# Block-sparse attention and eight experts: expert tiles of 128 instead of 256 slots, the last seven under nested conditions

## The chip, the cores and the metric

One program on one core of a Trainium2 chip. The metric is the device time of the program in microseconds (us). The engines are TensorE (PE; its weight loads are a row of their own, PEld), VectorE (DVE), ScalarE (ACT), GpSimd (POOL) and SyncE (SP, which issues the transfers of weights). Matrix products read SBUF and write PSUM; VectorE and ScalarE carry results from PSUM back to SBUF.

## The reference

Two stages, all in f32. The first is masked attention (4 batches, 8 heads, 768 positions, heads of 64); the second sends each of the 3072 tokens, of width 512, to one of 8 experts:

```
xn = x / (norm(x) + 1e-6);  en = expert_emb / (norm(expert_emb) + 1e-6)
logits = xn @ en.T / tau
expert_idx = argmax(logits, axis=1)
gate_w = softmax(logits)[expert_idx]
for e in range(8):
    mask = expert_idx == e
    h = maximum(x[mask] @ w1[e], 0.0)          # w1[e]: 512 x 1024
    out[mask] = gate_w[mask] * (h @ w2[e])     # w2[e]: 1024 x 512
```

The inputs come from a fixed seed. With them the eight experts get 813, 192, 322, 753, 256, 320, 192 and 224 tokens.

## The kernel before

The program runs in four stretches: attention (`attention_fast`) with the router of each batch behind it (`route`), which writes the tokens and their gate weight as rows of 513 numbers to `x_dram`; then `dispatch`, which sorts the tokens into slots; then `experts`; last a condition on `good` (L635), whose body repeats everything in a safer form and is skipped with these inputs.

`dispatch` gives each expert whole tiles of `G` = 256 slots. Which expert a tile belongs to stands in `k.expert`, which token a slot holds in `k.slot` (an empty slot points at a row of zeros). Since the number of tiles that the experts fill is known only on the chip, the kernel always runs the most there can be, `NG` = (3072 + 8·255) // 256 = 19. With the counts above the experts fill 4 + 1 + 2 + 3 + 1 + 2 + 1 + 1 = 15 of them; the other 4 work on rows of zeros.

`experts` (L585) calls `fetch(i + 1)` and `expert_tile(i)` in turn. `fetch` (L465) loads the expert's number into a register of SP, and SP issues one transfer for `w1` (L469) and one for `w2` (L471), 2 MB each, into pools of two buffers; GpSimd gathers two times 128 rows of `x_dram` (L476). `expert_tile` (L485) makes on TensorE, one after the other: 8 transposes of 128x128 into PSUM (`xg_ps`, L491), 32 products `hp` with 256 columns (L502: 8 blocks of the hidden width times 4 of the depth), and two times 8 products `yp` with 512 columns (L510). The trace counts each f32 product as two instructions (a weight load and a matmul each), so a tile has 8 pairs of transposes, 64 pairs of `hp` and 32 of `yp`. Half of the transposed tokens is copied by DVE (L494), half by ACT (L495). `hp` uses a new PSUM buffer for each four blocks; ACT takes the relu of the first two blocks (L504) and DVE that of the other two (L505). DVE scales `yp` by the gate (L513), and GpSimd scatters the rows to the output (L515).

The Tile framework sets the order on each engine by a schedule, and adds a wait wherever two engines touch the same tile; the order below is what it made.

Of the kernel before, what the change touches and what calls it, by code (L numbers as in the profile page):

```python
# [406 lines left out]
def dispatch(k):  # L407

    nc, p = k.nc, k.dp
    cp = k.small.tile([P, 512], F32, name="cp", tag="small")  # L410
    nc.tensor.matmul(cp[:, 0:E], lhsT=k.ones, rhs=k.seen[:, NT, :], start=True, stop=True)
    cnt = p.tile([P, E], F32, name="cnt")
    nc.vector.tensor_copy(out=cnt, in_=cp[:, 0:E])

    more = p.tile([P, E, N // G], F32, name="more")
    nc.vector.tensor_tensor(out=more, in0=cnt.unsqueeze(2).broadcast_to([P, E, N // G]),
                            in1=k.by_g.unsqueeze(1).broadcast_to([P, E, N // G]), op=ALU.is_gt)
    need = p.tile([P, E], F32, name="need")
# [36 lines left out]

    ps = k.small.tile([P, 512], F32, name="slot_ps", tag="small")
    for t in range(NT):
        lane = p.tile([P, P], F32, name="lane_oh", bufs=4)
        nc.vector.tensor_scalar(out=lane, in0=k.lane, scalar1=low[:, t:t + 1], scalar2=None, op0=ALU.is_equal)
        nc.tensor.matmul(ps[:, 0:NS], lhsT=lane, rhs=val[:, t, :], start=(t == 0), stop=(t == NT - 1))  # L460
    k.slot = k.const.tile([P, NS], I32, name="slot")
    nc.vector.tensor_scalar(out=k.slot, in0=ps[:, 0:NS], scalar1=float(N), scalar2=None, op0=ALU.add)  # L462


def fetch(k, i):  # L465
    nc = k.nc
    e = nc.values_load(k.expert[0:1, i:i + 1], engines=(mybir.EngineType.SP,), min_val=0, max_val=E - 1)
    w1 = k.wp.tile([P, ND, F], F32, name="w1", tag="w1")
    nc.sync.dma_start(out=w1, in_=k.w1[bass.ds(e, 1), :, :].rearrange("o (c p) f -> p (o c) f", p=P))  # L469
    w2 = k.wp.tile([P, NF, DM], F32, name="w2", tag="w2")  # L470
    nc.sync.dma_start(out=w2, in_=k.w2[bass.ds(e, 1), :, :].rearrange("o (c p) m -> p (o c) m", p=P))  # L471
    xs = []
    for s in range(GS):
        x = k.gp.tile([P, XW], F32, name="xg", tag="xg")
        t = i * GS + s
        nc.gpsimd.indirect_dma_start(  # L476
            out=x[:, :], out_offset=None, in_=k.x_dram[:, :],
            in_offset=bass.IndirectOffsetOnAxis(ap=k.slot[:, t:t + 1], axis=0),
            bounds_check=N, oob_is_err=False,
        )  # L480
        xs.append(x)
    k.fetched[i] = (w1, w2, xs)


def expert_tile(k, i):  # L485
    nc = k.nc
    w1, w2, xs = k.fetched.pop(i)
    ps = k.big.tile([P, ND, GS, P], F32, name="xg_ps", tag="big")
    for d in range(ND):
        for s in range(GS):  # L490
            nc.tensor.transpose(ps[:, d, s, :], xs[s][:, d * P:(d + 1) * P], k.ident)  # L491
    xt = k.mp.tile([P, ND, G], F32, name="xgt", tag="xgt")
    half = ND // 2
    nc.vector.tensor_copy(out=xt[:, 0:half], in_=ps[:, 0:half].rearrange("p d s t -> p d (s t)"))  # L494
    nc.scalar.copy(out=xt[:, half:ND], in_=ps[:, half:ND].rearrange("p d s t -> p d (s t)"))  # L495

    h = k.mp.tile([P, NF, G], F32, name="h", tag="h")
    for f0 in range(0, NF, 4):
        hp = k.big.tile([P, 4, G], F32, name="hp", tag="big")
        for f in range(4):  # L500
            for d in range(ND):
                nc.tensor.matmul(hp[:, f, :], lhsT=w1[:, d, (f0 + f) * P:(f0 + f + 1) * P], rhs=xt[:, d, :],  # L502
                                 start=(d == 0), stop=(d == ND - 1))
        nc.scalar.activation(h[:, f0:f0 + 2], hp[:, 0:2], ACT.Relu)  # L504
        nc.vector.tensor_scalar(out=h[:, f0 + 2:f0 + 4], in0=hp[:, 2:4], scalar1=0.0, scalar2=None, op0=ALU.max)  # L505

    for s in range(GS):
        yp = k.small.tile([P, DM], F32, name="yp", tag="small")
        for f in range(NF):
            nc.tensor.matmul(yp, lhsT=h[:, f, s * P:(s + 1) * P], rhs=w2[:, f, :],  # L510
                             start=(f == 0), stop=(f == NF - 1))
        y = k.gp.tile([P, DM], F32, name="y", tag="y")
        nc.vector.tensor_scalar(out=y, in0=yp, scalar1=xs[s][:, DM:XW], scalar2=None, op0=ALU.mult)  # L513
        t = i * GS + s
        nc.gpsimd.indirect_dma_start(  # L515
            out=k.out[:, :], out_offset=bass.IndirectOffsetOnAxis(ap=k.slot[:, t:t + 1], axis=0),
            in_=y[:, :], in_offset=None, bounds_check=N - 1, oob_is_err=False,
        )
# [66 lines left out]
def experts(n):  # L585
    with ExitStack() as ctx:
        n.wp = ctx.enter_context(n.tc.tile_pool(name="wp", bufs=2))
        n.gp = ctx.enter_context(n.tc.tile_pool(name="gp", bufs=4))
        n.mp = ctx.enter_context(n.tc.tile_pool(name="mp", bufs=2))
        fetch(n, 0)  # L590
        for i in range(NG):
            if i + 1 < NG:
                fetch(n, i + 1)
            expert_tile(n, i)


@with_exitstack
def kernel(
# [23 lines left out]
    n.small = ctx.enter_context(tc.tile_pool(name="small", bufs=2, space=PSUM))  # L622
# [3 lines left out]
    with ExitStack() as attn:  # L626
        attention_fast(n, attn)
    n.big = ctx.enter_context(tc.tile_pool(name="big", bufs=3, space=PSUM))
    with tc.tile_pool(name="dp", bufs=1) as n.dp:
        dispatch(n)  # L630
        count_good(n)
    experts(n)

    good = n.nc.values_load(n.good[0:1, 0:1], min_val=0, max_val=N * H)
    with tc.If(good < N * H):  # L635
        n.exact = True
        with tc.tile_pool(name="const_x", bufs=1) as n.const_x, ExitStack() as attn:
            attention_exact(n, attn)
        with tc.tile_pool(name="dp_x", bufs=1) as n.dp:
            dispatch(n)  # L640
        experts(n)


# [30 lines left out]
```

## Time and profile before

| what | value |
|---|---|
| median of three runs | 1157.51 us (1157.3 to 1158.6) |
| the profiled execution | 1155.99 us, its span 1154.3 us |
| mean granted TensorE clock | 0.953 |
| PE busy | 1091.7 us (95%) |
| stretch of the experts | from 568 us to the end |

The page gives, for one execution, the busy time of each engine, the span in 40 slices, the chain of work that ended last and the costliest groups of instructions. A granted clock of 1.00 is 2.4 GHz, 0.50 is 1.2 GHz. A DMA share of 1.0 means that all 16 DMA engines were moving packets.

### The profile page before, as it was taken

The numbers are of one execution on the slowest core, as the hardware profiler recorded it, in microseconds if no ns is written. First come the engines' busy times: TensorE is split into PE (matmuls) and PEld (weight loads), VectorE is DVE, ScalarE is ACT, GpSimd is POOL, SyncE is SP. The second block draws the span as 40 slices with busy tenths as digits, with TensorE's granted clock in tenths as the row PEclk, the third lists the DMA queues.
The fourth block names the chain that finished last, engine by engine and source line by source line (L and its number), as shares of the span: only waits on it lengthen the run. The fifth ranks groups of instructions, "written<-read, shape, count | busy, mean of one in ns | idle before, by whom it ended". The sixth has DMA issues, their size and how long they took to land.

```text
span 1154.3 us, 12005 instructions
## 1 busy us (share of the span) xinstructions
PE 1091.7 (95%) x4938; PEld 617.5 (53%) x4938; DVE 309.8 (27%) x526; ACT 235.6 (20%) x370; POOL 93.3 (8%) x125
## 2 busy tenths in 40 slices
PE   5999999999999999998499999999999999999995
PEld 2444454445344454436466666666666666666662
DVE  3444434443344434434501111111111111111110
ACT  2443423343344413342000000000000000000000
POOL 1000010000000010000101111111111111111100
PEclk9999979998899969998589999999999999999998
DMA  6111111111211110000385554454444444454400
GB/s 151 42 42 41 42 69 41 42 42 28 96 41 42 42 55 14 1 2 7 144 305 182 182 182 165 170 174 159 173 171 173 175 177 166 175 181 164 165 1 3
DMA packets 91159, 122.05 MB, mean 106 GB/s; under 512 B 53324, under 2 KB 57420, under 8 KB 90582
## 3 DMA queue, kind: packets, MB, share of 16 engines
q1 hardware_dynamic: 85014, 104.90, 27.4%
q0 software_dynamic: 6080, 16.28, 4.0%
q8 instruction: 41, 0.67, 0.2%
q14 instruction: 24, 0.20, 0.0%
HBM read 108.56 MB, written 16.27 MB: 108 GB/s over the span
## 4 chain that ended last, share of the span: by engine, by line
PE 93%; DVE 2%; issue 2%; DMA 1%; SPq 1%; POOL 0%; POOLq 0%
PE hp L502 23%; PE yp L510 23%; PE sc L275 15%; PE av L295 14%; PE sc L272 5%; PE back L317 3%; PE turn L257 3%; PE lg L368 3%; PE xg_ps L491 2%; PE back L313 1%; DVE xgt L494 1%; PE xt_ps L363 1%; DMA xg<-x_dram,slot 1%; DVE xt L365 1%; SPq L173 1%
## 5 line engine op out<-in xcount | busy, mean ns | idle before, releaser
L502 PE MATMUL hp<-xgt,w 128*128 128x256 f32 x1216 | 270.1, 383 | 14.9 <-DVE xgt L494 14.1
L510 PE MATMUL yp<-w,h 128*128 128x512 f32 x608 | 264.0, 592 | 0.0
L502 PEld LDWEIGHTS hp<-xgt,w 128*128 128x128 f32 x1216 | 231.3, 191 | 50.7 <-DVE xgt L494 18.4
L278 ACT ACTIVATE e<-sc 128x768 f32<-128x768 f32 x192 | 155.4, 809 | 288.7 <-PE sc L275 288.7
L275 PE MATMUL sc<-qt,kt 64*128 64x384 f32 x768 | 192.7, 557 | 0.0
L510 PEld LDWEIGHTS yp<-w,h 128*128 128x128 f32 x608 | 115.5, 190 | 137.3 <-issue 136.3
L295 PE MATMUL av<-e,vld 128*64 128x384 f32 x768 | 173.5, 525 | 0.0
L293 DVE TENSOR_TENSOR esum<-esum,e 128x768 f32<-128x768 f32 x128 | 122.4, 956 | 106.0 <-ACT e L278 106.0
L505 DVE TENSOR_SCALAR h<-hp 128x512 f32<-128x512 f32 x38 | 26.3, 691 | 270.7 <-ACT h L504 270.7
L513 DVE TENSOR_SCALAR y<-yp,xg 128x512 f32<-128x512 f32 x38 | 28.5, 751 | 221.6 <-PE yp L510 221.6
L295 PEld LDWEIGHTS av<-e,vld 128*64 128x64 f32 x768 | 39.3, 137 | 81.9 <-issue 64.0
L275 PEld LDWEIGHTS sc<-qt,kt 64*128 64x128 f32 x768 | 62.7, 192 | 35.9 <-issue 35.8
L515 POOL DMA_INDIRECT out_dram<-y,slot x38 | 38.5, 1014 | 485.2 <-DVE y L513 485.2
L504 ACT ACTIVATE h<-hp 128x512 f32<-128x512 f32 x38 | 22.7, 597 | 247.7 <-PE hp L502 247.7
L272 PEld LDWEIGHTS <-kmask 24*128 24x128 bf16 x384 | 18.3, 91 | 102.7 <-issue 102.2
L495 ACT COPY xgt<-xg_ps 128x512 f32<-128x512 f32 x19 | 11.1, 585 | 299.9 <-DVE xgt L494 299.9
L272 PE MATMUL sc<-qmask,kmask 24*128 24x384 bf16 x384 | 66.5, 340 | 0.0
L291 DVE TENSOR_TENSOR esum<-e 128x768 f32<-128x768 f32 x32 | 30.7, 958 | 110.9 <-ACT e L278 110.9
L317 PEld LDWEIGHTS back<-ones,esum 128*128 128x128 f32 x384 | 45.4, 192 | 0.0
L317 PE MATMUL back<-ones,esum 128*128 128x1 f32 x384 | 44.7, 243 | 0.0
L354 POOL TENSOR_TENSOR nrm<-nrm,half 128x6 f32<-128x6 f32 x4 | 5.3, 1327 | 485.7 <-ACT sq L353 485.7
L476 POOL DMA_INDIRECT xg<-x_dram,slot x38 | 39.2, 1030 | 31.5 <-DVE slot L462 20.3
(124 smaller groups left out, 423.7 us busy)
## 6 DMA issues: line engine op xcount, KB each, us to landing
w<-in_moe_w_dram SPq DMA_DIRECT2D x38, 2048.0 KB, 9.3
x_dram<-x SPq DMA_DIRECT2D x4, 1539.0 KB, 5.8
kld<-in_k_dram SPq DMA_DIRECT2D x32, 192.0 KB, 3.1
qld<-in_q_dram SPq DMA_DIRECT2D x32, 192.0 KB, 3.2
vld<-in_v_dram SPq DMA_DIRECT2D x16, 384.0 KB, 3.1
xg<-x_dram,slot POOLq DMA_INDIRECT x38, 6.5
out_dram<-y,slot POOLq DMA_INDIRECT x38, 2.8
x_dram<-zero SPq DMA_DIRECT2D x1, 2.0 KB
```

Of the source, the lines that this page charges most:

```text
L257: nc.tensor.transpose(ps[:, c * P:(c + 1) * P], src[:, lo + c].rearrange("p h d -> p (h d)"), k.ident)
L272: nc.tensor.matmul(ps[:, h, 0:HALF], lhsT=k.kmask[32 * h:32 * h + NB, keys], rhs=k.qmask[32 * h:32 * h + NB, queries], start=True, stop=False)
L275: nc.tensor.matmul(ps[:, h, 0:HALF], lhsT=kt[D * h:D * (h + 1), keys], rhs=qt[D * h:D * (h + 1), queries], start=False, stop=True)
L278: nc.scalar.activation(e, ps[:, :, 0:HALF], ACT.Exp)
L293: nc.vector.tensor_tensor(out=k.esum, in0=k.esum, in1=e, op=ALU.add)
L295: nc.tensor.matmul(k.av[D * h:D * (h + 1), 0:HALF], lhsT=v[:, h, kc, :], rhs=e[:, h, :], start=(kc == 0), stop=(kc == NC - 1))
L317: nc.tensor.matmul(ps[:, i:i + 1], lhsT=esum[:, h, t * P:(t + 1) * P], rhs=k.ones[:, 0:1], start=True, stop=True)
L368: nc.tensor.matmul(lg[:, c, :], lhsT=xt[:, (c - c2) * ND + d, :], rhs=k.en[:, d, :], start=(d == 0), stop=(d == ND - 1))
L476: nc.gpsimd.indirect_dma_start(out=x[:, :], out_offset=None, in_=k.x_dram[:, :], in_offset=bass.IndirectOffsetOnAxis(ap=k.slot[:, t:t + 1] ...
L502: nc.tensor.matmul(hp[:, f, :], lhsT=w1[:, d, (f0 + f) * P:(f0 + f + 1) * P], rhs=xt[:, d, :], start=(d == 0), stop=(d == ND - 1))
L510: nc.tensor.matmul(yp, lhsT=h[:, f, s * P:(s + 1) * P], rhs=w2[:, f, :], start=(f == 0), stop=(f == NF - 1))
L515: nc.gpsimd.indirect_dma_start(out=k.out[:, :], out_offset=bass.IndirectOffsetOnAxis(ap=k.slot[:, t:t + 1], axis=0), in_=y[:, :], in_offse ...
```

## The change

`G` becomes 128, so one tile is 128 slots, `GS` is 1, and `NG` is (3072 + 8·127) // 128 = 31. The 3072 tokens fill at least 24 tiles whatever the router says, so 24 tiles run always; each of the other 7 runs under a condition that stands inside the one before it, `used > i`, where `used` is the number of tiles that the experts fill, worked out in `dispatch`. With the counts above that is 7 + 2 + 3 + 6 + 2 + 3 + 2 + 2 = 27.

The pools of the expert stage give way to named buffers (`ring`): three for `w1` and for `w2`, four for the gathered rows and for `y`, two for the rest. `fetch` runs two tiles ahead instead of one. A tile's 4 transposes are copied by DVE alone. All 8 blocks of `hp` share one PSUM tile; ACT takes the relu of its first half as soon as that is there, DVE that of the second. PSUM pools are opened anew for each stage, since the rings take all of it.

```diff
-G = 256
+G = 128
...
+    k.used = k.const.tile([P, 1], I32, name="used")
+    nc.vector.tensor_scalar(out=k.used, in0=end[:, E - 1:E], scalar1=float(NG), scalar2=None, op0=ALU.min)
...
+def ring(k, name, i, n, pool, shape):
+    key = name, i % n
+    if key not in k.rings:
+        k.rings[key] = pool.tile(shape, F32, name=f"{name}_{i % n}")
+    return k.rings[key]
...
-    w1 = k.wp.tile([P, ND, F], F32, name="w1", tag="w1")
+    w1 = ring(k, "w1", i, 3, k.wp, [P, ND, F])
...
-    ps = k.big.tile([P, ND, GS, P], F32, name="xg_ps", tag="big")
+    x = xs[0]
+    ps = ring(k, "xg_ps", i, 2, k.eps, [P, ND, P])
     for d in range(ND):
...
+        nc.tensor.transpose(ps[:, d, :], x[:, d * P:(d + 1) * P], k.ident)
+    xt = ring(k, "xgt", i, 2, k.wp, [P, ND, P])
+    nc.vector.tensor_copy(out=xt, in_=ps)
+
+    hp = ring(k, "hp", i, 2, k.eps, [P, NF, P])
+    h = ring(k, "h", i, 2, k.wp, [P, NF, P])
+    half = NF // 2
+    for f in range(NF):
+        for d in range(ND):
+            nc.tensor.matmul(hp[:, f, :], lhsT=w1[:, d, f * P:(f + 1) * P], rhs=xt[:, d, :],
+                             start=(d == 0), stop=(d == ND - 1))
+        if f == half - 1:
+            nc.scalar.activation(h[:, 0:half], hp[:, 0:half], ACT.Relu)
+    nc.vector.tensor_scalar(out=h[:, half:NF], in0=hp[:, half:NF], scalar1=0.0, scalar2=None, op0=ALU.max)
...
+        fetch(n, 1)
+        for i in range(N // G):
+            fetch(n, i + 2)
             expert_tile(n, i)
+        used = n.nc.values_load(n.used[0:1, 0:1], min_val=0, max_val=NG)
+        with ExitStack() as more:
+            for i in range(N // G, NG):
+                more.enter_context(n.tc.If(used > i))
+                if i + 2 < NG:
+                    fetch(n, i + 2)
+                expert_tile(n, i)
```

On TensorE two tiles of before stand like this in the middle of the expert stage (`w_...` are the weights, a row's last number is how often it repeats):

```order
L491 MATMUL xg_ps<-ident,xg 128x128 x8
L502 MATMUL hp<-xgt,w_4023 128x256 x32
L510 MATMUL yp<-w_4025,h 128x512 x16
L491 MATMUL xg_ps<-ident,xg 128x128 x8
L502 MATMUL hp<-xgt,w_4124 128x256 x32
L510 MATMUL yp<-w_4126,h 128x512 x16
```

And like this the changed kernel's third tile (`hp_3746`, `w_2`) and the first half of its fourth, with what each row waits for:

```order
L510 MATMUL hp_3746<-xgt_3744,w_2_3731 128x128 [waits DMAHW4_49]
L510 MATMUL hp_3746<-xgt_3744,w_2_3731 128x128 x15
L501 MATMUL xg_ps_3739<-ident,xg_3699 128x128 [waits DMASW5_49]
L501 MATMUL xg_ps_3739<-ident,xg_3699 128x128 x3
L510 MATMUL hp_3746<-xgt_3744,w_2_3731 128x128 [waits Activation_49]
L510 MATMUL hp_3746<-xgt_3744,w_2_3731 128x128 x15
L518 MATMUL yp_3782<-w_2_3733,h_3747 128x512 [waits DMAHW5_49]
L518 MATMUL yp_3782<-w_2_3733,h_3747 128x512 x3
L518 MATMUL yp_3782<-w_2_3733,h_3747 128x512 [waits DVE_49]
L518 MATMUL yp_3782<-w_2_3733,h_3747 128x512 x3
L510 MATMUL hp_3819<-xgt_3817,w_0_3695 128x128 [waits DMAHW6_49]
```

The transposes of a later tile have moved from between two tiles into the middle of `hp`, and the second half of `hp` now waits for ScalarE.

At the end of the expert stage TensorE of before goes from its 19th tile straight to the condition on `good`:

```order
L491 MATMUL xg_ps<-ident,xg 128x128 x8
L502 MATMUL hp<-xgt,w_5437 128x256 x32
L510 MATMUL yp<-w_5439,h 128x512 x16
L634 TENSOR_LOAD good
L635 COMPARE_AND_BRANCH
```

In the changed kernel the 24th tile is followed by the load of `used` and the first condition; here are that and two conditional tiles:

```order
L599 TENSOR_LOAD used
L600 COMPARE_AND_BRANCH
L501 MATMUL xg_ps_3739<-ident,xg_3699 128x128 x4
L510 MATMUL hp_3746<-xgt_3744,w_0_3695 128x128 x32
L518 MATMUL yp_3782<-w_0_3697,h_3747 128x512 x8
L600 COMPARE_AND_BRANCH
L501 MATMUL xg_ps_3812<-ident,xg_3717 128x128 x4
L510 MATMUL hp_3819<-xgt_3817,w_1_3713 128x128 x32
L518 MATMUL yp_3855<-w_1_3715,h_3820 128x512 x8
```

Nothing is moved across a condition: a conditional tile's transposes stand directly ahead of its products. Every engine has such a branch for each of the seven tiles.

## Rows read from the trace of the kernel before

**Rows 1.** Page: busy time by engine (share, instructions), then the chain's shares.

```profile
PE 1091.7 (95%) x4938; PEld 617.5 (53%) x4938; DVE 309.8 (27%) x526; ACT 235.6 (20%) x370; POOL 93.3 (8%) x125
...
PE 93%; DVE 2%; issue 2%; DMA 1%; SPq 1%; POOL 0%; POOLq 0%
```

**Rows 2.** Chain in order of time, the last tiles: start us, length us, what.

```profile
1097.71 13.73 PE yp L510 x32
1111.45 0.89 PE xg_ps L491 x8
1113.11 14.08 PE hp L502 x64
1127.19 13.75 PE yp L510 x32
```

**Rows 3.** Busy time by stretch: engines, then granted clock, DMA share, GB/s.

```profile
612.10:641.57 29.47, 28.69 (x104) 19.09 (x104) 3.58 (x5) 1.76 (x3) 4.10 (x5) 1.00 0.51 178
...
614.00:618.00 4.00, 4.00 (x20) 3.54 (x19) 0.00 (x0) 0.00 (x0) 0.00 (x0) 1.00 1.02 383
...
576.00:580.00 4.00, 2.20 (x8) 1.54 (x8) 0.69 (x1) 0.00 (x0) 0.00 (x0) 0.50 1.03 373
568.00:611.00 43.00, 33.41 (x113) 22.54 (x113) 3.54 (x6) 1.78 (x3) 6.30 (x6) 0.80 0.76 281
```

**Rows 4.** Timeline of TensorE, three places: start us, length us, what.

```profile
97.11 1.42 PEld L317 LDWEIGHTS back<-ones,esum 128*128 128x128 f32 x12
...
558.66 9.51 PEld L460 LDWEIGHTS slot_ps<-val,lane_oh 128*128 128x128 f32 x44
...
610.28 1.04 PE L491 MATMUL xg_ps<-ident,xg 128*128 128x128 f32 x8
```

**Rows 5.** Timeline, all engines, between two tiles and inside hp.

```profile
610.48 0.75 DVE L513 TENSOR_SCALAR y<-yp,xg 128x512 f32<-128x512 f32 x1 [6.12 <-PE yp L510]
...
611.36 0.69 DVE L494 COPY xgt<-xg_ps 128x512 f32<-128x512 f32 x1
...
612.10 0.94 PEld L502 LDWEIGHTS hp<-xgt,w 128*128 128x128 f32 x5 [1.02 <-DVE xgt L494]
...
619.31 0.60 ACT L504 ACTIVATE h<-hp 128x512 f32<-128x512 f32 x1 [6.65 <-PE hp L502]
```

**Rows 6.** SP's waits (total us, times, longest), and the page's weight transfers.

```profile
SPq L469 <- PE hp L502: 260.5, 17, 18.2
...
w<-in_moe_w_dram SPq DMA_DIRECT2D x38, 2048.0 KB, 9.3
```

**Rows 7.** Timeline, all engines: dispatch, then the first expert tile.

```profile
552.77 1.13 DVE L446 TENSOR_TENSOR ge<-pos,by_p 128x936 f32<-128x936 f32 x1
...
573.01 1.00 POOL L476 DMA_INDIRECT xg<-x_dram,slot  x1 [0.30 <-issue]
...
577.52 1.75 PE L491 MATMUL xg_ps<-ident,xg 128*128 128x128 f32 x7 [0.89 <-DMA xg<-x_dram,slot]
...
580.10 16.61 PE L502 MATMUL hp<-xgt,w 128*128 128x256 f32 x64 [0.83 <-issue]
```

**Rows 8.** The condition on good (L635) by instruction: ns min/median/max, first and last start.

```profile
L635 SPq EVENT_SEMAPHORE  x9: 17/17/17, 1087.4 to 1091.5; - x9
L635 POOLq EVENT_SEMAPHORE  x5: 17/42/43, 1145.0 to 1145.3; - x5
L635 SPq COMPARE_BRANCH  x1: 53/53/53, 1082.4 to 1082.4; - x1
...
L635 DVEq COMPARE_BRANCH  x1: 72/72/72, 1141.6 to 1141.6; - x1
L635 POOLq COMPARE_BRANCH  x1: 53/53/53, 1142.3 to 1142.3; - x1
L635 DVEq EVENT_SEMAPHORE  x1: 21/21/21, 1144.5 to 1144.5; - x1
L635 POOLq INC_SWDGE_SEM  x1: 1708/1708/1708, 1145.4 to 1145.4; - x1
```

More of the change, by code (lines that the diff above doesn't have):

```diff
@@ L461, in dispatch @@
     k.slot = k.const.tile([P, NS], I32, name="slot")
-    nc.vector.tensor_scalar(out=k.slot, in0=ps[:, 0:NS], scalar1=float(N), scalar2=None, op0=ALU.add)
+    nc.vector.tensor_scalar(out=k.slot, in0=ps[:, 0:NS], scalar1=float(N), scalar2=0.0, op0=ALU.add, op1=ALU.max)
+def ring(k, name, i, n, pool, shape):
[3 more added lines that the diff above has]
+    return k.rings[key]
 def fetch(k, i):
@@ L467, in fetch @@
     e = nc.values_load(k.expert[0:1, i:i + 1], engines=(mybir.EngineType.SP,), min_val=0, max_val=E - 1)
[L468 removed]
+    w1 = ring(k, "w1", i, 3, k.wp, [P, ND, F])
     nc.sync.dma_start(out=w1, in_=k.w1[bass.ds(e, 1), :, :].rearrange("o (c p) f -> p (o c) f", p=P))
[L470 removed]
+    w2 = ring(k, "w2", i, 3, k.wp, [P, NF, DM])
     nc.sync.dma_start(out=w2, in_=k.w2[bass.ds(e, 1), :, :].rearrange("o (c p) m -> p (o c) m", p=P))
@@ L473, in fetch @@
     for s in range(GS):
-        x = k.gp.tile([P, XW], F32, name="xg", tag="xg")
+        x = ring(k, "xg", i, 4, k.wp, [P, XW])
         t = i * GS + s
@@ L487, in expert_tile @@
     w1, w2, xs = k.fetched.pop(i)
-    ps = k.big.tile([P, ND, GS, P], F32, name="xg_ps", tag="big")
+    x = xs[0]
+    ps = ring(k, "xg_ps", i, 2, k.eps, [P, ND, P])
     for d in range(ND):
[L490 to L518, printed above, removed]
+        nc.tensor.transpose(ps[:, d, :], x[:, d * P:(d + 1) * P], k.ident)
@@ new lines, in expert_tile @@
+    nc.vector.tensor_scalar(out=h[:, half:NF], in0=hp[:, half:NF], scalar1=0.0, scalar2=None, op0=ALU.max)
+    yp = ring(k, "yp", i, 2, k.eps, [P, DM])
+    for f in range(NF):
+        nc.tensor.matmul(yp, lhsT=h[:, f, :], rhs=w2[:, f, :], start=(f == 0), stop=(f == NF - 1))
+    y = ring(k, "y", i, 4, k.wp, [P, DM])
+    nc.vector.tensor_scalar(out=y, in0=yp, scalar1=x[:, DM:XW], scalar2=None, op0=ALU.mult)
+    nc.gpsimd.indirect_dma_start(
+        out=k.out[:, :], out_offset=bass.IndirectOffsetOnAxis(ap=k.slot[:, i:i + 1], axis=0),
+        in_=y[:, :], in_offset=None, bounds_check=N - 1, oob_is_err=False,
+    )
@@ L582, in attention_exact, with experts @@
                 route(n, (u - 1) // (H * NC) - 1)
[L585 to L589, printed above, removed]
+def experts(n, tag=""):
+    n.rings = {}
+    with n.tc.tile_pool(name="wp" + tag, bufs=1) as n.wp, n.tc.tile_pool(name="eps" + tag, bufs=1, space=PSUM) as n.eps:
         fetch(n, 0)
-        for i in range(NG):
-            if i + 1 < NG:
-                fetch(n, i + 1)
+        fetch(n, 1)
+        for i in range(N // G):
+            fetch(n, i + 2)
             expert_tile(n, i)
+        used = n.nc.values_load(n.used[0:1, 0:1], min_val=0, max_val=NG)
[5 more added lines that the diff above has]
+                expert_tile(n, i)
 @with_exitstack
@@ L621 @@
     n.const = ctx.enter_context(tc.tile_pool(name="const", bufs=1))
-    n.small = ctx.enter_context(tc.tile_pool(name="small", bufs=2, space=PSUM))
     n.x_dram = tc.dram_tile([N + 1, XW], F32, name="x_dram")
     n.dens = n.const.tile([P, 2 * B * NPAIR, 2 * NQ], F32, name="dens")
[L626 to L631, printed above, removed]
+    with tc.tile_pool(name="small", bufs=2, space=PSUM) as n.small:
+        with ExitStack() as attn:
+            attention_fast(n, attn)
+        with tc.tile_pool(name="dp", bufs=1) as n.dp:
+            dispatch(n)
+            count_good(n)
     experts(n)
@@ L636 @@
         n.exact = True
[L637 to L641, printed above, removed]
+        with tc.tile_pool(name="small_x", bufs=2, space=PSUM) as n.small:
+            with ExitStack() as attn:
+                n.const_x = attn.enter_context(tc.tile_pool(name="const_x", bufs=1))
+                n.big = attn.enter_context(tc.tile_pool(name="big", bufs=3, space=PSUM))
+                attention_exact(n, attn)
+            with tc.tile_pool(name="dp_x", bufs=1) as n.dp:
+                dispatch(n)
+        experts(n, "_x")
 _INS = ['q', 'k', 'v', 'sampled_blocks', 'moe_expert_emb', 'moe_tau', 'moe_w1', 'moe_w2']
```

## The prediction

> **What bounds the kernel now.** I read the page first: PE is busy for 95% of the span, and the chain of work that ended last is 93% PE [rows 1]. So time is won only by giving TensorE less to do, or lost by giving it something to wait for. The change leaves the attention alone; it acts from 568 us on. There the chain in order of time shows one tile after the other with a fixed rhythm: 13.73 us of `yp`, 1.66 us from the first transpose to the first product of `hp` (1111.45 to 1113.11, of which the 8 transposes take 0.89), 14.08 us of `hp` [rows 2]. That is 29.47 us, and a stretch of exactly that length shows clock 1.00 and a DMA share of 0.51 at 178 GB/s [rows 3]: the weights come twice as fast as they are used. SP confirms it: it waited 260 us for `hp` to set its buffers free, and never the other way round [rows 6]. 19 such tiles are 560 us, nearly half the time.
>
> **The work itself.** Per slot, a 128-slot tile has the same `yp` work, the same transposes, and the same matmul columns in `hp`. What does not halve are the weight loads of `hp`: still 64 pairs, now with 128 columns each. The question is whether a pair costs half as much.
> A pass of `hp` with 256 columns takes 14.08 / 64 = 0.220 us, one of `yp` with 512 columns 13.73 / 32 = 0.429 [rows 2]; time follows the columns, and the 128-column weight load ahead of each pass adds nothing visible. With 128 columns the pass alone would be 0.110. The load alone: 12 loads ahead of passes with one column take 1.42 us, 0.118 each with the tail of the last, and 44 loads at half clock (ahead of 38 columns, whose passes are hidden) 9.51, 0.216 each, so 0.108 at full clock [rows 4]. Load and pass are therefore about equal, 0.108 to 0.118, and if they go on side by side a pair takes 0.112: 64 pairs are 7.17 us. 16 passes of `yp` are 16 x 0.429 = 6.86, four transposes half of 0.89, 0.44 [rows 2]. Sum 14.47 us of TensorE work in a tile. Loads and passes of equal length side by side have no row of their own; the nearest are 8 transposes, whose 128-column loads and passes take 1.04 us together, 0.13 each with the tail, so they do go side by side [rows 4].
> The Trainium skill's page "TensorE: Matmul & The Clock Gate" (Part 3, The mechanism) says that a weight load overlaps a running matmul only where the two use different row groups of the array. By that rule each of these 128-row loads would stand in front of its pass. The rows just read speak against it; what it would cost is the first rival.
>
> **How many tiles.** The token counts of the inputs (813, 192, 322, 753, 256, 320, 192, 224) need 27 tiles of 128; 24 run always, 3 under conditions, 4 are skipped. Before, 19 tiles of 256 ran, 38 of today's size.
>
> **What is added inside a tile: a wait for ACT.** All of `hp` is one PSUM tile now, and in the order TensorE's second half of `hp` waits for ACT's relu of the first half. ACT's relu takes 0.60 us; the hand-over is read from the same turn with DVE: transposes end at 611.32, copy 611.36 to 612.05, loads go on at 612.10 [rows 5]. With the drain of the last product ahead (1.04 against 0.89, [rows 2, 4]) and the first load behind it a bare wait is about 1.0 us. Covered by what the schedule put there: nothing in tiles 0, 1 and 23, four transposes (0.44) in tiles 2 and 3, 0.22 in tile 22, six pairs (0.66) in 12 tiles and eight pairs of the next `hp` (0.90) in 6. What is left open is 3 x 1.0 + 2 x 0.56 + 0.78 + 12 x 0.34 + 6 x 0.10 = 9.6 us. In return the 1.66 us between two tiles is gone in the first 24, since transposes and copy now stand a tile ahead. DVE has a copy, a relu of the same shape and a scaling per tile, 0.69 + 0.69 + 0.75 = 2.1 of 14.5 us, and is not late [rows 5]. So 24 x 14.47 + 9.6 = 356.9, less 16 transposes (1.8) that come before the first `hp`: 355.1 us.
>
> **The conditional tiles.** Here nothing is moved ahead, so each pays the turn and the whole ACT wait. With four transposes instead of eight the turn gains only 0.1 of the 1.66, because DVE scales the last `y` (610.48 to 611.23) before it copies [rows 5]: 1.56. Per tile 14.47 - 0.44 + 1.56 + 1.0 = 16.6, three are 49.8. The branch that is not taken has no row. Lower end nothing: the compare itself took 53 to 72 ns [rows 8]. Upper end 2.9 us each, as long as DVE stood still after the one jump that the trace has (1141.6 to 1144.5) [rows 8]; behind it DVE's copy and so `hp` are queued. I take nothing, because that row is a jump to far-off code, and keep 3 x 2.9 = 8.7 for the range. On SP the same branch may cost 5.0 us (1082.4 to 1087.4) [rows 8], with the weights of two tiles ahead queued behind it: they have the time.
>
> **Loading.** Three weight buffers and a `fetch` two tiles ahead: SP issues `w1` when the `hp` three tiles back is done, some 6.9 + 2 x 14.8 = 36 us before it is needed; landing took 9.3 us [rows 6]. Bytes per tile are 2 x 2.10 of weights, 0.26 gathered and 0.26 scattered, 4.72 MB in 14.8 us, 319 GB/s, against 373 and 383 GB/s where the share was full [rows 3]. It fits, with a sixth to spare. GpSimd issues two transfers of about 1 us per tile; no bound.
>
> **Start and dispatch.** In `dispatch` some arrays shrink (936 elements, 1.13 us [rows 7], become 768) and two double, with one more small operation: nothing, within 0.5 us. TensorE now has the transposes of four tiles ahead of the first `hp`, so it waits for the fourth gather. The second landed at 577.5; the fourth is issued two spacings of 1.30 us after it, so 580.1, and four transposes at half clock (1.75 / 7 us or a little less each) give 581.0 instead of 580.1 [rows 7]. At half clock the first `hp` lost 16.61 - 14.08 = 2.5 us [rows 2, 7]; the same again.
>
> **The end.** After tile 26 every engine jumps out of the fourth condition and then three short steps over the other branches' leftovers. On GpSimd the known jump took 2.7 us (1142.3 to 1145.0) and the semaphore step behind it 1.7 [rows 8]; the short jumps have no row, 0 to 2.7 each, I take 0.3: 2.7 + 1.7 + 0.9 = 5.3, upper end 12.5. The Trainium skill's "Advanced Engine Details and Errata" (Control Flow Timing) gives 51 ns for a branch; by it the three would be 0.15 instead of 0.9. From the last `yp` (1127.19 + 13.75) to the span's end before were 13.4 us [rows 2]; they remain, so 18.7.
>
> **The sum.** 581.0 + 2.5 + 355.1 + 49.8 = 988.4 at the last `yp`; + 18.7 = 1007.1 of span. Around the span lay 1155.99 - 1154.3 = 1.7, and the median is 1.5 above the profiled execution: 1010.
>
> **Rivals.**
> A, slower: load and pass do not overlap when both are short. Then a pair is 0.112 + 0.110 = 0.222 instead of 0.112, 64 x 0.110 = 7.0 more per tile, 27 tiles 190 us: 1200 us. It decides from a pair of 0.197 on (147 us / 27 / 64 above 0.112). Against it: the loads under 256 columns and the transposes. For it: no row has load and pass of equal length in a long series.
> B, the DMA becomes the bound. 27 tiles need 127.4 MB; TensorE gives them about 405 us, so it decides below 314 GB/s. The lowest row while transfers ran thick is 281 [rows 3], which gives 453 us and 1057 in the end. Against it: that row had idle DMA in it (share 0.76).
> C, branches are dear: every engine stands still at each condition, taken or not. Three entries at 2.9 to 5.0 and three short jumps at 2.7 are 17 to 23 us more: 1027 to 1033, and with a late gather or two 1040.
> D, the conditions don't skip: all 31 tiles run, 4 x 16.6 = 66 more: 1076.
>
> **Chances.** Forecast 0.80, A 0.06, B 0.05, C 0.06, D 0.03. Its own range: a pair of 0.108 (-7), no cost at the end (-5) and waits half as long (-6) give 992; a pair of 0.118 (+10) and dear branches (+16) 1036; taking in C, 992 to 1042. Measurement tells 0.2% here, 2.3 us. Faster: all but A; a part of A (0.01) would end near break-even.
>
> **What would show it.** In the profile after: passes of `hp` 0.112 apart on PE (A: 0.22); idle time on TensorE put down to ACT of 0.1 to 0.6 us per tile; a DMA share near 0.8 with SP still waiting for PE (B: PE waits for the weights); three tiles of 16.6 us behind the 24th (C: over 19); 27 scalings `y`, not 31 (D); 18 to 19 us from the last `yp` to the end. A pair that costs more than 0.12, or TensorE at clock 0.50 inside the stretch, would make the forecast wrong.

## The result and the profile after

The changed kernel takes 1000.43 us (median of four runs, 999.39 to 1002.77) against 1157.76 us before: a ratio of 0.8643, with an interval of 0.8626 to 0.8661. The prediction said 1010 us, within 992 to 1042. The profiled execution took 999.39 us, with a span of 997.6.

These lines of the page after answer to [rows 1] and to the transfers in [rows 6]: busy time by engine; the chain's shares; then groups (line, engine, operation, count, busy us, mean ns of one, idle time before them and what ended it); and the weights' transfers (count, KB, us to landing).

```profile
PE 942.3 (94%) x5230; PEld 542.6 (54%) x5230; DVE 298.0 (30%) x513; ACT 218.0 (22%) x340; POOL 73.1 (7%) x105
...
PE 89%; issue 5%; DVE 2%; DMA 1%; SPq 1%; ACT 0%; POOL 0%; POOLq 0%; ACTq 0%
...
L510 PE MATMUL hp<-xgt,w 128*128 128x128 f32 x1728 | 204.2, 277 | 9.1 <-ACT h L513 4.9
L518 PE MATMUL yp<-w,h 128*128 128x512 f32 x432 | 189.9, 592 | 0.0
...
L520 DVE TENSOR_SCALAR y<-yp,xg 128x512 f32<-128x512 f32 x27 | 20.3, 750 | 158.6 <-PE yp L518 158.6
...
w<-in_moe_w_dram SPq DMA_DIRECT2D x58, 2048.0 KB, 9.4
```

PE is still the bound. It has 149 us less to do (1091.7 before), which is nearly all of the 157 us. `y` is scaled 27 times, so 27 tiles ran, and 1728 / 27 = 64 pairs of `hp` are left in each. The kernel fetches 58 / 2 = 29 tiles of weights, since it runs two tiles ahead.

The chain in order of time, in the middle of the tiles that run always (start us, length us, what), answers to [rows 2]:

```profile
676.97 6.87 PE yp L518 x16
683.83 3.57 PE hp L510 x32
687.41 0.66 PE xg_ps L501 x6
688.06 0.03 issue
688.09 3.84 PE hp L510 x32
691.93 6.87 PE yp L518 x16
698.80 8.10 PE hp L510 x72
```

Where `hp` runs on, 32 pairs take 3.57 us, 0.1116 each; 16 passes of `yp` take 6.87. Behind the wait for ACT the chain gives the same 32 pairs 3.84: the wait itself is covered by transposes, but the end of the last transpose ahead of it and the first weight load behind it are not.

Two stretches, three tiles that run always and the three conditional ones (engines' busy time, then clock, DMA share, GB/s), answer to [rows 3]:

```profile
669.76:713.77 44.01, 43.95 (x255) 31.99 (x254) 6.31 (x9) 1.79 (x3) 6.13 (x6) 1.00 0.90 323
934.04:984.30 50.26, 44.93 (x252) 31.72 (x250) 6.19 (x9) 1.79 (x3) 6.15 (x6) 1.00 0.68 240
```

A tile that runs always takes 14.67 us, a conditional one 16.75. The timeline of TensorE at the first tile and at a conditional one (start us, length us, what, and in brackets the idle time before it and its releaser; [rows 7] for the first):

```profile
579.42 4.22 PE L510 MATMUL hp<-xgt,w 128*128 128x128 f32 x32
584.45 3.84 PE L510 MATMUL hp<-xgt,w 128*128 128x128 f32 x32 [0.81 <-ACT h L513]
...
950.66 0.60 PE L501 MATMUL xg_ps<-ident,xg 128*128 128x128 f32 x4
952.26 3.84 PE L510 MATMUL hp<-xgt,w 128*128 128x128 f32 x32 [1.00 <-DVE xgt L503]
956.84 3.84 PE L510 MATMUL hp<-xgt,w 128*128 128x128 f32 x32 [0.74 <-ACT h L513]
```

The conditional tile shows both open turns, 1.00 us for DVE's copy and 0.74 for ACT's relu. The profile shows no idle time of TensorE for the branch itself. Last, the instructions of the conditions by instruction (ns min/median/max, first and last start; L600 are the seven new ones, L645 the one on `good`, which was L635 in [rows 8]) and of the program's end (L682):

```profile
L600 PEldq COMPARE_BRANCH  x5: 65/86/3692, 928.6 to 984.5; - x5
L600 DVEq COMPARE_BRANCH  x5: 43/47/67, 934.7 to 985.2; - x5
L600 POOLq INC_SWDGE_SEM  x1: 1301/1301/1301, 985.5 to 985.5; - x1
...
L645 POOLq EVENT_SEMAPHORE  x6: 17/30/43, 990.2 to 990.7; - x6
...
L645 POOLq COMPARE_BRANCH  x1: 55/55/55, 987.7 to 987.7; - x1
...
L682 POOLq DRAIN  x3: 46/107/4636, 992.1 to 997.3; - x3
```

### The profile page after: what moved, and what is told of

It reads as the page before. It is cut to its first block, busy times and chain, and to the rows that moved or that the text cites. A ratio compares the mean times of both kernels' runs of the same rounds, so it can differ in the third digit from the quotient of the medians.

```text
span 997.6 us, 12554 instructions
## 1 busy us (share of the span) xinstructions
PE 942.3 (94%) x5230; PEld 542.6 (54%) x5230; DVE 298.0 (30%) x513; ACT 218.0 (22%) x340; POOL 73.1 (7%) x105
## 4 chain that ended last, share of the span: by engine, by line
PE 89%; issue 5%; DVE 2%; DMA 1%; SPq 1%; ACT 0%; POOL 0%; POOLq 0%; ACTq 0%
PE sc L275 18%; PE hp L510 18%; PE yp L518 17%; PE av L295 16%; PE sc L272 5%; PE back L317 4%; PE turn L257 3%; PE lg L368 3%; PE back L313 2%; PE xg_ps L501 1%; PE slot_ps L462 1%; PE xt_ps L363 1%; DMA out_dram<-y,slot 1%; SPq L173 1%; DVE xt L365 0%
## 5 line engine op out<-in xcount | busy, mean ns | idle before, releaser
L510 PEld LDWEIGHTS hp<-xgt,w 128*128 128x128 f32 x1728 | 199.5, 192 | 25.4 <-issue 11.0
L510 PE MATMUL hp<-xgt,w 128*128 128x128 f32 x1728 | 204.2, 277 | 9.1 <-ACT h L513 4.9
L518 PE MATMUL yp<-w,h 128*128 128x512 f32 x432 | 189.9, 592 | 0.0
L518 PEld LDWEIGHTS yp<-w,h 128*128 128x128 f32 x432 | 80.0, 190 | 90.4 <-issue 90.4
L513 ACT ACTIVATE h<-hp 128x512 f32<-128x512 f32 x27 | 16.1, 597 | 412.7 <-PE hp L510 383.7
L272 PEld LDWEIGHTS <-kmask 24*128 24x128 bf16 x384 | 18.2, 91 | 102.3 <-issue 101.8
L520 DVE TENSOR_SCALAR y<-yp,xg 128x512 f32<-128x512 f32 x27 | 20.3, 750 | 158.6 <-PE yp L518 158.6
L514 DVE TENSOR_SCALAR h<-hp 128x512 f32<-128x512 f32 x27 | 18.7, 691 | 160.9 <-PE hp L510 160.9
L521 POOL DMA_INDIRECT out_dram<-y,slot x27 | 27.5, 1017 | 352.9 <-DVE y L520 338.5
L368 PEld LDWEIGHTS lg<-en,xt 128*128 128x128 f32 x192 | 29.4, 242 | 6.3 <-DVE xt L365 4.6
L486 POOL DMA_INDIRECT xg<-x_dram,slot x29 | 29.9, 1032 | 29.2 <-DVE slot L464 20.6
```

Source lines behind the costliest of these rows:

```text
L272: nc.tensor.matmul(ps[:, h, 0:HALF], lhsT=k.kmask[32 * h:32 * h + NB, keys], rhs=k.qmask[32 * h:32 * h + NB, queries], start=True, stop=False)
L368: nc.tensor.matmul(lg[:, c, :], lhsT=xt[:, (c - c2) * ND + d, :], rhs=k.en[:, d, :], start=(d == 0), stop=(d == ND - 1))
L486: nc.gpsimd.indirect_dma_start(out=x[:, :], out_offset=None, in_=k.x_dram[:, :], in_offset=bass.IndirectOffsetOnAxis(ap=k.slot[:, t:t + 1] ...
L510: nc.tensor.matmul(hp[:, f, :], lhsT=w1[:, d, f * P:(f + 1) * P], rhs=xt[:, d, :], start=(d == 0), stop=(d == ND - 1))
L518: nc.tensor.matmul(yp, lhsT=h[:, f, :], rhs=w2[:, f, :], start=(f == 0), stop=(f == NF - 1))
```

## The experiments

**All 31 tiles, no condition (e1).** It separates the smaller tile from the skipping.

```diff
-        for i in range(N // G):
-            fetch(n, i + 2)
+        for i in range(NG):
+            if i + 2 < NG:
+                fetch(n, i + 2)
             expert_tile(n, i)
-        used = n.nc.values_load(n.used[0:1, 0:1], min_val=0, max_val=NG)
...
```

> The changed kernel without conditions: all 31 tiles of 128 run. Theory (the time follows the tiles that run, 14.67 us for one in a row, and a condition only costs the turn that the schedule can't hide, 16.72 against 14.67 us): 4 more tiles at 14.7 are +59, three conditional tiles become plain ones, -6: 1000 + 53 = 1053 us, and the stretch from the last yp to the end stays 13.3 us although no branch is left but the one on good. Rival (the branches cost more than the turn, for instance in the end stretch): under 1045. Rival (the DMA engines, busy 0.90 of the time, give way over a longer stretch): over 1060.

It took 1053.18 us (1047.59 to 1053.92), ratio 0.9087 [0.9058, 0.9116]. So the conditions are worth 53 us, four tiles skipped less what three conditional tiles pay, and they do skip: rival D of the prediction is out. The end was not as I expected: from the last `yp` (1038.7) to the end of the span (1050.9) there are 12.2 us, 1.1 less than with conditions.

**Tiles of 256, but under conditions (e2).** The other half alone: fixed buffers and conditions, with 15 of 19 large tiles run. `expert_tile` does the work of a tile as it did before the change, with its copies and relus shared by DVE and ACT (its code is not shown here), and the weights are fetched one tile ahead.

```diff
-G = 128
+G = 256
...
-    w1 = ring(k, "w1", i, 3, k.wp, [P, ND, F])
+    w1 = ring(k, "w1", i, 2, k.wp, [P, ND, F])
...
```

> The kernel before with one part of the change: its 256-slot tiles in fixed buffers (two of each weight, fetch one ahead as before), 12 always and 7 under nested conditions, of which 15 run. Theory (what is won is work on empty slots): 4 tiles of 29.47 us less, 1157.5 - 118 = 1040 us; the rest of the gain, 40 us, is then that 27 small tiles hold what 15 large ones (30 small) held. Rival (the gain comes from the buffers three deep and the schedule, not from the skipping): 1120 or more.

It took 1042.79 us (1041.84 to 1044.31), ratio 0.9013 [0.8993, 0.9033]. Skipping the four empty tiles of 256 gives 115 of the 157 us; the other 42 come with the smaller tiles, 27 of 128 instead of 15 of 256 (30 halves). Not all of the 42 is work in the tiles: here 18.2 us pass from the last `yp` (1022.2) to the end of the span (1040.4), 4.8 more than in the profile after.

**`hp` in two PSUM tiles (e3).** TensorE's second half no longer waits for ACT's relu of the first.

```diff
-    hp = ring(k, "hp", i, 2, k.eps, [P, NF, P])
+    hps = [ring(k, f"hp{j}", i, 2, k.eps, [P, half, P]) for j in range(2)]
...
-            nc.scalar.activation(h[:, 0:half], hp[:, 0:half], ACT.Relu)
-    nc.vector.tensor_scalar(out=h[:, half:NF], in0=hp[:, half:NF], scalar1=0.0, scalar2=None, op0=ALU.max)
+            nc.scalar.activation(h[:, 0:half], hps[0], ACT.Relu)
+    nc.vector.tensor_scalar(out=h[:, half:NF], in0=hps[1], scalar1=0.0, scalar2=None, op0=ALU.max)
```

> The changed kernel with hp as two PSUM tiles of four blocks each, so that the second half of hp no longer waits for ScalarE; nothing else. The schedule then puts the transposes of two tiles ahead of every second hp again. Theory (in the 24 plain tiles the wait for ScalarE is covered by transposes and products put there, 4.9 us of idle in all, and three times 0.74 are open in the conditional tiles): the wait is gone, but the turn comes back open every second tile, 0.8 us ten times: 1000 - 6 + 8 = 1002, within 995 to 1006. Rival (the wait costs what the prediction gave it, 9.6 + 3 us, in full): 988.

It took 997.17 us (993.36 to 1000.56), ratio 0.8605 [0.8582, 0.8627]; the interval overlaps that of the changed kernel. The group of `hp` on its page shows why so little came of it:

```profile
L510 PE MATMUL hp<-xgt,w 128*128 128x128 f32 x1728 | 200.2, 277 | 8.8 <-DVE xgt L503 8.8
```

The wait for ACT is gone, and a wait of the same size for DVE's copy has taken its place: the schedule now puts the transposes of two tiles together between two tiles, with nothing behind them.

**The same, with the transposes placed by hand (e4).** `turn_tile` is a tile's transposes and copy; it stands in the middle of the `hp` of the tile before, in the conditional tiles too.

```diff
+        if f == half - 1 and ahead:
+            turn_tile(k, i + 1)
...
+        turn_tile(n, 0)
...
-            expert_tile(n, i)
+            expert_tile(n, i, ahead=True)
...
-                expert_tile(n, i)
+                expert_tile(n, i, ahead=i + 1 < NG)
```

> As e3_split_hp, and the transposes and the copy of tile i+1 are written in the middle of hp of tile i, in the plain and in the conditional tiles. Theory: TensorE has neither wait in any tile; plain tiles stay at 14.67 us (7.36 + 6.87 + 0.44), the first and last ones lose 3.5 us of idle, the conditional ones go from 16.72 to 14.7, -6: 991 us. Rival (the DMA engines hold the rhythm at 14.67, and a tile can't be shorter on average): 997 or more with PE waiting for the weights.

It took 987.16 us (982.12 to 988.93), ratio 0.8525 [0.85, 0.855]: faster than before, and 1.3% faster than the changed kernel, whose interval lies wholly above this one. Its timeline of TensorE over a conditional tile, and a stretch of those that run always:

```profile
940.51 3.73 PE L516 MATMUL hp<-xgt,w 128*128 128x128 f32 x32
944.09 0.60 PE L500 MATMUL xg_ps<-ident,xg 128*128 128x128 f32 x4
...
954.96 3.73 PE L516 MATMUL hp<-xgt,w 128*128 128x128 f32 x32
```

```profile
669.00:712.00 43.00, 43.00 (x252) 31.52 (x251) 6.40 (x9) 1.79 (x3) 5.77 (x7) 1.00 0.91 326
```

No idle time is left, under conditions as without, and a tile takes 954.96 - 940.51 = 14.45 us; the tiles that run always, which I had expected to stay at 14.67, have become shorter too. A condition costs TensorE nothing, therefore; what made the conditional tiles of the changed kernel longer were the two open turns.

**64 columns in `hp` (e5).** It asks which of load and pass sets the pair.

```diff
-            nc.tensor.matmul(hp[:, f, :], lhsT=w1[:, d, f * P:(f + 1) * P], rhs=xt[:, d, :],
+            nc.tensor.matmul(hp[:, f, 0:64], lhsT=w1[:, d, f * P:(f + 1) * P], rhs=xt[:, d, 0:64],
```

> The first product of every tile streams 64 token columns instead of 128; the second half of each tile's hidden values is left at zero, so that half of the tokens get no expert output. Every load of 128 rows stays. Theory (the load of the weights sets the pair of load and pass, which took 0.115 us with 128 columns): the pair stays near 0.11 us, each tile loses 0.3 us at most, and the time is between 985 and 1000 us. Rival (the pass sets the pair): the pair falls to about 0.06 us, 64 pairs lose 3.5 us in each of 27 tiles, and the time would fall by some 95 us to about 905 us, or as far as the transfers of the weights allow (4.72 MB at 353 GB/s is 13.4 us per tile, so about 965 us).

It took 1119.94 us in its one run, 120 us more than the changed kernel with half the columns. Neither theory had that. TensorE's timeline in an early tile, and two stretches of it:

```profile
600.64 3.68 PE L510 MATMUL hp<-xgt,w 128*128 128x64 f32 x32
605.01 6.58 PE L510 MATMUL hp<-xgt,w 128*128 128x64 f32 x32 [0.69 <-ACT h L513]
```

```profile
592.00:645.00 53.00, 51.47 (x218) 36.21 (x217) 6.12 (x9) 1.32 (x3) 6.16 (x6) 0.78 0.81 296
600.60:604.40 3.80, 3.72 (x33) 3.54 (x31) 0.75 (x1) 0.04 (x1) 2.06 (x2) 1.00 1.04 418
605.00:611.40 6.40, 6.39 (x33) 6.39 (x34) 0.00 (x0) 0.00 (x0) 0.00 (x0) 0.55 1.04 410
```

The question asked has its answer in the first row: at clock 1.00, 32 pairs with 64 columns take 3.68 us where 128 columns took 3.73. The load sets the pair, and with 64 columns nothing is won. The rest is mostly the clock. From 592 to 645 us TensorE shows as busy for 51.47 of 53 us and waited for nothing but ACT, 0.69 us at a time; its granted clock was 0.78 in the mean, about 1.00 in one half of `hp` and 0.55 in the next. In the same stretch of the changed kernel, which also has waits for ACT, the row reads `592.00:645.00 53.00, 51.79 (x300)` with clock 1.00. What differs in `hp` is that each pass has half the columns, beside a load of the same length; the schedule has also moved the transposes, from the middle of `hp` to behind it. `hp` and `yp` together were 90 us longer busy than after (255.7 + 228.0 against 204.2 + 189.9), `yp` through the clock alone. Another 26 us are longer waits for ACT, DVE and gathers. What made the clock fall is not shown further than by this one comparison, of one profile each.

**1 MB more per fetch (e6).** It asks how much room the transfers have.

```diff
+    junk = ring(k, "junk", i, 2, k.wp, [P, NF // 2, DM])
+    nc.sync.dma_start(out=junk, in_=k.w2[bass.ds(e, 1), 0:DM, :].rearrange("o (c p) m -> p (o c) m", p=P))
```

> Each fetch of a tile's weights also moves 1 MB of the same weights into a buffer that nothing reads; nothing else changes. A tile then moves 5.77 MB. Theory (the queues held 0.90 of their time at 320 GB/s in the plain tiles, so they can move about 353 GB/s): a tile needs 16.3 us, PE waits for weights, and the time rises by about 36 us to 1036 us (1025 to 1050). Rival (the queues can move the 373 to 383 GB/s that they showed in the router and early stages): a tile needs 15.1 to 15.5 us, and the time rises by 10 to 20 us to 1010 to 1020 us.

It took 1161.21 us in its one run, far outside both. Its timeline of TensorE, TensorE's waits for gathers from 600 to 1100 us (total, times, longest), and the stretch of its first tiles:

```profile
787.53 1.09 PE L503 MATMUL xg_ps<-ident,xg 128*128 128x128 f32 x4 [5.77 <-DMA xg<-x_dram,slot]
788.42 6.23 PE L512 MATMUL hp<-xgt,w 128*128 128x128 f32 x32
...
801.35 3.73 PE L512 MATMUL hp<-xgt,w 128*128 128x128 f32 x32
```

```profile
PE xg_ps L503 <- DMA xg<-x_dram,slot: 115.8, 20, 6.3
```

```profile
600.00:650.00 50.00, 35.45 (x181) 27.28 (x180) 4.08 (x6) 1.79 (x3) 5.13 (x5) 0.86 1.04 406
```

TensorE did not wait for weights but for gathered rows, 5.8 us at a time in 20 of its tiles, and with the waits the clock fell: from 781.80 to 787.50 TensorE stood still, and from 786.80 to 793.60 the granted clock was 0.50, so that 32 pairs of `hp` took 6.23 instead of 3.73. The instruction order tells where that comes from. Four buffers hold gathered rows, so tile 4's gather can be issued only when tile 0 has been scaled. In the changed kernel tile 4's transposes stand in the middle of tile 2's `hp`; here the schedule put them into tile 1's, a whole tile earlier. TensorE comes to them while the gather is on its way, and all that is queued behind them, `hp` of a tile whose data had long been there, waits with them. The gathers themselves were no slower: they landed 6.9 us after their issue (median), 7.4 in the changed kernel. And the first tiles moved 406 GB/s, more than I had thought the queues could.

**The same with later transposes (e9).** To tell the placing of the transposes from the bytes, e4's kernel got the extra 1 MB; there the schedule put tile 4's transposes behind tile 1's `yp`.

> The kernel of e4_split_ahead (987.2 us) with the extra 1 MB per fetch of e6_dma_plus1mb. In PE's order the transposes of a tile now stand half a first product and a second product later than in e6 (10.6 us), so that the gather that they read has had that much longer. Theory (in e6 PE waited for gathers that had been issued too late before transposes that stood too early, 5.7 us in each tile, and the queues had room): that wait is gone, the queues move 5.77 MB in about 14.5 us at the 406 GB/s that they showed in e6's first tiles, and the time is 985 to 1010 us. Rival (the queues are full at 353 GB/s): 16.3 us per tile with PE waiting for weights, and the time is about 1037 us. Second rival (the extra transfers themselves slow the gathers): the wait for the gathers stays and the time is above 1100 us.

It took 991.65 us in its one run: 170 us less than e6 with the same bytes. 300 us of its expert stage, then two rows of TensorE's timeline, `hp` of one tile and of the next:

```profile
620.00:920.00 300.00, 300.00 (x1736) 218.75 (x1735) 42.76 (x63) 12.47 (x21) 41.84 (x41) 1.00 1.04 405
```

```profile
641.48 7.31 PE L518 MATMUL hp<-xgt,w 128*128 128x128 f32 x64
...
655.93 7.31 PE L518 MATMUL hp<-xgt,w 128*128 128x128 f32 x64
```

TensorE is busy for all of 300.00 us at 14.45 us a tile, while the queues move 405 GB/s at a share of 1.04. So the transfers have room for a quarter more than the 323 GB/s of the changed kernel, and e6's time came from where the transposes stood. (e9 differs from e6 by e4's two PSUM tiles as well; without the extra 1 MB, those and the placing by hand were worth 13 us together.) I had read the room off wrongly: 323 GB/s at a share of 0.90 does not mean that 1.00 is 359. The Trainium skill's page "DMA: Bandwidth & Descriptors" (Where 436 GB/s comes from) names the memory's side, some 358 GB/s, as what binds a load into SBUF; the row of 405 GB/s is above it, and the measurement decides. It is nearer to the 425 that the page measured for one core with its neighbour idle.

**Two weight buffers, fetched one tile ahead (e7).**

```diff
-    w1 = ring(k, "w1", i, 3, k.wp, [P, ND, F])
+    w1 = ring(k, "w1", i, 2, k.wp, [P, ND, F])
...
-            fetch(n, i + 2)
+            fetch(n, i + 1)
```

> The weights have two buffers instead of three and are fetched one tile ahead instead of two. Theory (a fetch lands 8 to 10 us after its issue, which is less than the part of a tile that is left when its buffer comes free plus the next tile's gather and first product): most of it stays hidden and the time is within 3 to 10 us of 1000 us. Rival (the third buffer carries the transfers): the transfers come in bursts, each tile waits for its weights by 3 us or more, and the time is above 1080 us.

It took 999.05 us (997.24 to 1002.14), ratio 0.8637 [0.8614, 0.8661], the same as the changed kernel. TensorE's waits on weights in the whole stage:

```profile
PE hp L510 <- DMA w<-in_moe_w_dram: 0.3, 1, 0.3
```

That is the one such wait. The third buffer and the longer lead bring nothing here: a transfer lands 10.4 us after its issue in this run, and one tile of lead is 14.7.

**Work for POOL at the end (e8, e10).** In the profile after, the stretch from the last `yp` to the end is as long as before, though POOL has more to do in it. Either POOL's drain hides that, or it doesn't.

```diff
+    idle = n.const.tile([P, 1024], F32, name="idle")
+    for _ in range(4):
+        n.nc.gpsimd.memset(idle, 0.0)
```

> Four memsets of 128x1024 on POOL (POOL alone, of a buffer that nothing reads) stand after the last tile, where the conditions' rejoining steps are. Theory (POOL's last drain ends a fixed 11.4 us after the last scatter's issue, whatever POOL does in between): the stretch from the last second product's end to the span's end stays 13.3 us and the time stays at 1000 us. Rival (steps on POOL add to the tail, as the prediction had it): the stretch grows by the memsets' own time, some 4 us, and the time with it.

It took 1001.64 us in its one run, but says nothing of the end: the memsets depend on no data, and the schedule put them at the program's start. The second try reads the last `y`, so it can't be moved:

```diff
+        late = n.wp.tile([P, DM], F32, name="late")
+        for _ in range(4):
+            n.nc.gpsimd.tensor_copy(out=late, in_=n.rings[("y", (NG - 1) % 4)])
```

> Four copies of 128x512 on POOL of the last tile's y into a buffer that nothing reads stand behind the conditional tiles, between the last scatter and the program's last steps (in e8 the four memsets did not stand there, they ran at the program's start). Theory (POOL's drain at the end waits for the last scatter, and what POOL does before it is hidden): from the last second product's end to the span's end stays at 13.3 us, and the time at 1000 us. Rival (POOL's steps and its drain follow one another): the stretch grows by the copies' own time, 4 to 8 us.

It took 1006.41 us in its one run, span 1004.4. The copies by instruction, and the drain at its end:

```profile
L608 POOL COPY late<-y x4: 607/612/615, 991.7 to 993.7; 128x512 f32<-128x512 f32 x4
```

```profile
L685 POOLq DRAIN  x3: 46/107/4637, 998.9 to 1004.1; - x3
```

The last `yp` began at 981.80 (977.23 in the profile after), so that the end moved from 997.6 - 977.23 = 20.4 us behind it to 22.6. That is 2.2 of the copies' 2.6 us, and the drain took 4.64 us as after. My theory falls: POOL's steps at the end are not hidden, nearly all of their time adds up, only the copies were smaller than I had put them.

## Why the prediction was right, step by step

The forecast's own mechanism held, and the sum came out 9.5 us of span too high, 5.4 of them in one term, the end:

| step | predicted | measured |
|---|---|---|
| first `hp` starts | 581.0 | 579.42 |
| lost to half clock in the first `hp` | 2.5 | 0.5 (4.22 - 3.73) |
| the 24 tiles, without that | 355.1 | 354.1 (579.42 to 934.04, less 0.5) |
| three conditional tiles | 49.8 | 50.3 |
| from the last `yp` to the end | 18.7 | 13.3 (984.30 to 997.6) |
| span | 1007.1 | 997.6 |

**Tiles.** A pair of load and pass was put at 0.112 us, from rows in which no load and pass of equal length stood in series. It is 0.1116, and a tile without waits takes 14.45 us (e4, e9) against 14.47. Rival A, load and pass one after the other, is out: these loads of all 128 rows run beside passes of all 128 rows. That is not what the prediction drew from the Trainium skill's "TensorE: Matmul & The Clock Gate" (Part 3, The mechanism); the same section also lets a load go ahead into a background weight buffer, and with that the trace agrees.

**The wait for ACT.** Predicted were 9.6 us. Measured: 354.1 less 24 x 14.45, plus the 1.75 us of transposes ahead of the first `hp`, leaves 9.1. Size and make-up were right. Around tile 1, where nothing covers the wait, the chain has

```profile
588.29 6.87 PE yp L518 x16
...
603.26 6.87 PE yp L518 x16
```

From one `yp` to the next are 14.97 us; 64 pairs and 16 passes that run on take 7.14 + 6.87 = 14.01, so the bare wait cost 0.96 against the predicted 1.0. With six transposes as cover (676.97 to 691.93, in the chain above) 14.96 - 14.01 - 0.65 = 0.30 is left, against 0.34; with eight pairs of the next `hp` (691.93 to 706.90) 14.97 - 8.03 - 6.87 = 0.07, against 0.10. The timeline shows a smaller loss: in its brackets an uncovered wait is 0.69 to 0.81 us of idle time, and a covered one nothing or nearly so. It leaves out the end of the last product ahead and the first load behind, 0.27 us together (3.84 - 3.57), which the prediction had counted.

**Conditions.** 16.75 us per tile against 16.6, and nothing for the branch. Rival C is out: DVE's compare took 43 to 67 ns, and the exit that C made dear is the next paragraph's. On PEld one of the five branches took 3.7 us, the jump out of the fourth condition, but the profile shows no TensorE work delayed by it: it lasts from 978.3 to 982.0, while the last `yp` (977.23 to 984.3) still runs. e4 confirms that a condition costs TensorE no time.

**The end.** This is the term that was mis-sized, by 5.4 us: 5.3 us were added to the 13.4 of before, and nothing came. The steps that I added there were 2.7 for a jump, 1.7 for the semaphore step and 0.9 for short jumps. The first was far too dear for this kernel. The chain of after shows POOL leave the fourth condition, and the last scatter start right behind it:

```profile
985.10 0.05 POOLq L600
...
985.29 0.02 POOLq L600
...
985.33 1.00 POOL out_dram L521
```

That exit takes 0.2 us. It is not so cheap in every kernel: in e2 POOL left the same condition at 1023.04, and its steps there stretch to 1027.0:

```profile
L603 POOLq EVENT_SEMAPHORE  x4: 17/42/43, 1023.2 to 1027.0; - x4
```

That is most of why e2's end is 18.2 us long, near the 18.7 that the prediction had for this kernel. What makes the exit short or long is not shown. The far jump, on `good`, was there before and is in the 13.4 already. The semaphore step took 1.3, and of the three short steps the trace has one, 0.2 us from its start to the load of `good` (986.9 to 987.0). The Trainium skill's "Advanced Engine Details and Errata" (Control Flow Timing) gives some 51 ns for a branch without a compare and some 108 with one; this one has a compare and took 38 ns, and the measurement decides.

What is left adds 1.6 us: the drain began 5.2 us behind the last scatter before (1142.0 to 1147.2) and 6.8 after (985.3 to 992.1). And the drain was shorter, 4.6 us against 6.3. The longest drain of POOL in before, in e1 and in e7:

```profile
L669 POOLq DRAIN  x3: 40/107/6272, 1147.2 to 1154.0; - x3
```

```profile
L676 POOLq DRAIN  x3: 40/107/5128, 1044.9 to 1050.6; - x3
```

```profile
L681 POOLq DRAIN  x3: 46/107/4554, 995.0 to 1000.2; - x3
```

Its length goes with the number of gathers and scatters that POOL issued: 76 before, 62 in e1 and in e2 (5.13 us in both), 56 after and in e10 (4.64), 55 in e7. In each it is 0.083 us for one. The runs show the proportion, not the mechanism. The changed kernel issues 20 fewer than before, which is the 1.6 us. So POOL's end stood 11.4 us behind the last scatter's issue in both, by two changes that cancel by chance: the conditions add steps, and fewer, smaller tiles save drain, which the prediction put at nothing. e10 fits: the steps that it adds come on top, and the drain stays.

**Transfers.** B is out: with 323 GB/s the share was 0.90, and SP still waited for TensorE (158.0 us for `hp` and 132.7 for `yp` in the 24 tiles), as the prediction had it. "A sixth to spare" was too little; e9 shows a quarter. The step on loading counted on three buffers; two are enough (e7).

**Start.** The first `hp` came 1.6 us early, since the stretch ahead of `dispatch` ended earlier in this execution: its product in L401 starts at 545.2, at 546.9 before. The half clock cost 0.5 us instead of 2.5, and that belongs to this execution and not to the kernel. Here the granted clock was 0.50 from 579.42 to 580.40 and 0.99 from there to 583.60, so it rose 1.0 us into the first `hp`. In e8, which has the same expert stage, the first 32 pairs took 5.71 us, 2.0 more than the 3.73 at full clock:

```profile
579.94 5.71 PE L510 MATMUL hp<-xgt,w 128*128 128x128 f32 x32
```

The predicted 2.5 was read from one execution too; between these two runs the term differs by 1.5 us, and that it came out low here is chance.

## What to carry to other kernels

When the number of tiles is known only on the chip, run the certain ones in a straight line and nest the rest in conditions: entering a condition cost an engine less than 0.1 us here, and what a conditional tile really pays for are the turns that no schedule can fill across it, unless the code itself does the next tile's turn inside this one. A wait that other instructions cover still cost 0.3 us here, for the end of the product ahead and the first weight load behind, so two PSUM tiles and a turn put in the right place are worth more than a covered wait. The end of a program is worth a count of its own: here a gather or scatter saved was 0.083 us less in POOL's last drain. An instruction that is scheduled early makes all behind it wait: the same bytes took 1161 or 992 us depending on whether four small transposes stood before or after the time their gather needed.

## What the runs showed of the hardware

- A weight load of 128 rows and columns in f32 and a pass of 128 columns run side by side at 0.1116 us per pair; with 64 columns it is no faster: 32 pairs take 3.68 us by the timeline, where 32 with 128 columns take 3.73.
- With passes of 64 columns beside loads of 128 columns TensorE's granted clock went down and up between its two levels (1.00 and 0.55 in neighbouring halves of `hp`), with nothing but waits of 0.69 us between. With 128 columns and waits for ACT as well it held 1.00.
- The DMA queues held 405 GB/s for 300 us with this kernel's transfers; a share of 0.90 was 323 GB/s.
- POOL's last drain took 0.083 us for each gather and scatter that POOL had issued, at 55, 56, 62 and 76 of them (4.55 to 6.27 us).
- The far jump on `good` took POOL 2.5 us after (987.7 to 990.2), but 5.5 in e9 (976.5 to 982.0); in e4, which is e9 without the extra 1 MB, 2.6 (973.0 to 975.6). In after and in e4 the queues were nearly empty (shares of 0.14 and 0.06), in e9 full (1.03). The stretches of after and of e9 around it:

```profile
985.00:991.00 6.00, 0.00 (x0) 0.00 (x0) 0.05 (x1) 0.00 (x0) 1.00 (x1) 0.63 0.14 45
```

```profile
972.00:982.00 10.00, 1.17 (x3) 0.19 (x1) 0.75 (x1) 0.00 (x0) 1.00 (x1) 0.82 1.03 384
```

  The Trainium skill's page "Runtime: NRT & Kernel Launch" (Instruction fetch mechanics) says that a taken branch out of the fetched window waits for a DMA. The times agree with that; no run here separates it from other causes.
